# A DeltaNet layer followed by a gated feed-forward: first-layer steps as two tasks, quarter copies shared by two engines, and a new order of all tasks

## Chip, cores and metric

The kernel runs on one core of one Trainium2 chip. The metric is the device time of one execution in microseconds (us), the median of several runs; lower is better. A core has five engines that run side by side, each in the order of its own instruction list: TensorE (PE in the profile, its weight loads PEld), VectorE (DVE), ScalarE (ACT), GpSimd (POOL) and SyncE (SP, which here only issues DMAs).

## What is computed

```python
# attention: q, k, v of shape (4, 8, 768, 48), beta (4, 8, 768)
k_n = k / (norm(k) + 1e-6)
for t in range(768):
    y[t]  = q[t] @ state                       # state: 48 x 48 for each batch and head
    v_old = k_n[t] @ state
    state = state + beta[t] * outer(k_n[t], v[t] - v_old)
# feed-forward on x = y as 3072 tokens x 384
h = x @ w_in                                   # w_in: 384 x 2048
out = (h * cos(h)) @ w_out                     # w_out: 2048 x 384
```

All of it is float32; in the kernel the weights come in as 64-bit words and are made into float32 on the chip.

## The kernel before

**Chunks.** The 768 steps are cut into 24 chunks of 32 (`NU`, `C`). Within a chunk the recurrence is a triangular system. For each chunk n: `turn` transposes keys and queries (TensorE, L541, copied out by ScalarE at L555; from chunk 8 on by DMA and VectorE instead); `gram` multiplies them (L578), VectorE scales the product into `g` and `tt` (L589, L612); `inverse` inverts the triangular matrices of a pair of chunks column by column on GpSimd (L688, L695; the first pair on VectorE), going out to DRAM and back with `gram_put`, `gram_get`, `put` and `get` on SP's queue.

**The chain from chunk to chunk.** `state` (`through_state`, L745) multiplies the state so far by keys and queries into the PSUM tile `p_kq`. `old` (`old_values`, L757) copies the part that belongs to the keys into the tile `rhs`, four copies on ScalarE, one for each batch: a batch owns 32 of the 128 partitions (a quarter). `right` (`right_side`, L764) subtracts it from v on VectorE. The first four chunks solve in two halves: `solve_half` (L774), `half_out` (ScalarE, L784), `between` (L774), `between_out` (VectorE, L792), `solve` (L808); later chunks solve at once (L814). `solve_out` (VectorE, L822) makes u, `update` (L835) its product with the keys, `update_out` (VectorE, L845 for the first chunk, L843 after) adds that to the state. `within` (L852) finishes y in `p_kq`, and `within_out` (L865) copies it to the tile `y`, again in four quarters on ScalarE. The tiles `rhs` and `y` share one buffer. For the first four chunks `features` (L873) and `features_out` (ScalarE, L880) transpose y into the feed-forward's input `x_ffn`; later chunks go through VectorE and DRAM.

**Feed-forward.** Two chunks make a pair p of 256 tokens. Pairs 0 and 1 compute the first layer plainly: `hidden` (L924) fills one PSUM tile `p_h` of 128 x 512 with 12 matmuls, and there are 8 such steps for a pair, written (p, f) with f = 0, 2, ..., 14; f below 8 belongs to the pair's first chunk, the others to the second. A step's tile then goes through `turns` (ScalarE, L962), `rest` (VectorE, L969), `cos` (ScalarE, L978) and `gate` (VectorE, L987). Three PSUM banks (tag "h") hold such tiles. Pair 0's second layer is plain as well (`output`, L1130); all others use products of sums (`product`, L1187), and from pair 2 on the first layer is a chain of sums and products, too (`layer`, L1110). The sums of weights and of inputs are made on VectorE.

**Weights.** 28 loads (12 of `w_in`, 16 of `w_out`, `narrow_load`, L441) go through four buffers; each is worked on by `split` (ScalarE, L449, L451), `shift` (VectorE, L455, L460) and `add` (GpSimd, L464). `add` frees the buffer for a later load.

**Order.** Every piece of work is a task with a key, an engine, what it must follow, and the buffers that it makes and uses. The class `Order` takes a list of numbers, `LINE`, written out by hand or by a planner beforehand: the order in which all 2215 tasks are emitted. Each engine's own list is what remains of that order. The costs and due times given to `add` are for the planner; `Order.run` doesn't use them. It checks that a task's predecessors came before it and that buffers suffice. Where two engines touch one tile, the framework adds the waits; `pin` keeps each engine's instructions in the order emitted.

Of the kernel before, what the change touches and what calls it, by code (L numbers as in the profile page):

```python
# [197 lines left out]
def kernel(  # L198
# [45 lines left out]
    GATES = 8  # L244
    LEAD = 3
    MOVED = 4
    PLAIN_TURNS = 8
    DH = 32

    const = ctx.enter_context(tc.tile_pool(name="const", bufs=1))  # L250
# [28 lines left out]
    def by_parity(t):  # L279
        return t.rearrange("p (j a) i -> p a j i", a=2)  # L280
# [1468 lines left out]
```

## Time and profile before

| | us |
|---|---|
| runs, in order | 649.08, 651.08, 652.69 |
| median | 651.08 |
| profiled execution, whole | 655.38 |
| its span, first to last instruction | 653.3 |
| TensorE busy (10044 matmul records) | 596.1 |
| VectorE busy | 538.5 |
| ScalarE busy | 357.0 |
| GpSimd busy | 341.8 |

The span is what all views of the trace refer to; 2.1 us of the execution lie around it. A matmul of float32 shows as two records. The three runs and the profiled one are executions of one program, so a difference of one or two microseconds between single executions says nothing. The mean granted clock of TensorE was 0.993 of full speed. Of the span, TensorE is busy 91% and VectorE 82%.

### The profile page before, as it was taken

The numbers are of one execution on the slowest core, as the hardware profiler recorded it, in microseconds if no ns is written. First come the engines' busy times: TensorE is split into PE (matmuls) and PEld (weight loads), VectorE is DVE, ScalarE is ACT, GpSimd is POOL, SyncE is SP. The second block draws the span as 40 slices with busy tenths as digits, with TensorE's granted clock in tenths as the row PEclk, the third lists the DMA queues.
The fourth block names the chain that finished last, engine by engine and source line by source line (L and its number), as shares of the span: only waits on it lengthen the run. The fifth ranks groups of instructions, "written<-read, shape, count | busy, mean of one in ns | idle before, by whom it ended". The sixth has DMA issues, their size and how long they took to land.

```text
span 653.3 us, 24215 instructions
## 1 busy us (share of the span) xinstructions
PE 596.1 (91%) x10044; PEld 555.2 (85%) x10044; DVE 538.5 (82%) x1107; ACT 357.0 (55%) x658; POOL 341.8 (52%) x703
## 2 busy tenths in 40 slices
PE   4327868999999999999999999999999999999997
PEld 3216867887788999998999999999999999999996
DVE  6775666698989999999899999989998878778782
ACT  3434485774344565564666565655755646646340
POOL 5337457868847728738468487188681283000000
PEclk9999899999999999999999999999999999999999
DMA  8866745675465554534563545553413303110000
GB/s 187 188 120 163 185 100 115 148 143 83 86 106 83 104 90 84 100 75 82 99 108 71 119 65 106 103 91 71 93 38 67 78 15 66 43 39 25 1 25 24
DMA packets 237200, 58.65 MB, mean 90 GB/s; under 512 B 228644, under 2 KB 232116, under 8 KB 237092
## 3 DMA queue, kind: packets, MB, share of 16 engines
q1 hardware_dynamic: 234084, 56.24, 43.5%
q8 instruction: 79, 1.29, 0.8%
q10 hardware_dynamic: 2752, 0.43, 0.4%
q0 software_dynamic: 256, 0.44, 0.3%
q14 instruction: 29, 0.24, 0.1%
HBM read 42.65 MB, written 14.42 MB: 87 GB/s over the span
## 4 chain that ended last, share of the span: by engine, by line
PE 66%; DVE 13%; DMA 9%; ACT 5%; issue 3%; SPq 2%; POOL 1%; DVEq 0%; ACTq 0%; POOLq 0%
PE p_out L1187 23%; PE p_h L1110 23%; PE p_h L924 5%; PE p_kq L745 3%; PE p_s L835 3%; PE p_kq L852 2%; DVE p_h L1008 2%; PE p_u L814 2%; PE p_g L578 2%; DMA pairs<-in_moe_w_in_dram 2%; DMA z_dr<-z 1%; PE p_out L1130 1%; PE p_o L1187 1%; DVE g_ffn L987 1%; DVE turns L969 1%
## 5 line engine op out<-in xcount | busy, mean ns | idle before, releaser
L688 POOL TENSOR_TENSOR part<-z,gb 128x56 f32<-128x56 f32 (+25 forms) x325 | 130.8, 402 | 115.7 <-DMA gb<-g_dr 78.6
L695 POOL TENSOR_TENSOR z<-z,part 128x56 f32<-128x56 f32 (+25 forms) x325 | 136.9, 421 | 25.5
L1126 ACT COPY g_ffn<-p_h 128x512 f32<-128x512 f32 x140 | 78.9, 588 | 92.0 <-DVE p_h L1008 53.4
L1187 PE MATMUL p_out<-w_out,g_ffn 128*128 128x192 f32 x672 | 122.2, 329 | 0.6 <-DVE g L589 0.3
L1008 DVE TENSOR_TENSOR p_h<-p_h,g_ffn 128x512 f32<-128x512 f32 x140 | 96.8, 694 | 25.5 <-ACT g_ffn L1126 13.0
L1187 PEld LDWEIGHTS p_out<-w_out,g_ffn 128*128 128x128 f32 x672 | 107.8, 190 | 2.3 <-issue 0.5
L962 ACT ACTIVATE turns<-p_h,quarter_turn 128x512 int32<-128x512 f32 x96 | 66.0, 688 | 57.8 <-DVE p_h L1008 47.1
L1187 PE MATMUL p_out<-w_sum,g_ffn 128*128 128x192 f32 x496 | 90.8, 330 | 0.6 <-DVE o L1237 0.5
L978 ACT ACTIVATE turns<-turns,halfpi 128x512 f32<-128x512 f32 x96 | 69.1, 722 | 37.4 <-DVE turns L969 36.7
L1110 PE MATMUL p_h<-x_sum,w_in 128*128 128x128 f32 x640 | 83.4, 278 | 0.7 <-ACT g_ffn L1126 0.5
L1187 PEld LDWEIGHTS p_out<-w_sum,g_ffn 128*128 128x128 f32 x496 | 79.5, 190 | 1.9 <-DVE o L1237 0.9
L1110 PEld LDWEIGHTS p_h<-x_sum,w_in 128*128 128x128 f32 x640 | 78.1, 192 | 2.3 <-ACT g_ffn L1126 1.7
L969 DVE SCALAR_TENSOR_TENSOR turns<-p_h,turns 128x512 f32<-128x512 f32 x96 | 65.4, 682 | 9.6 <-ACT turns L962 8.8
L987 DVE TENSOR_TENSOR g_ffn<-turns,p_h 128x512 f32<-128x512 f32 x86 | 58.4, 679 | 9.2 <-ACT turns L978 9.2
L865 ACT COPY y<-p_kq 32x384 f32<-32x384 f32 x96 | 45.1, 470 | 37.5 <-PE p_kq L852 36.1
L1203 DVE TENSOR_TENSOR g_ffn<-g_ffn 128x512 f32<-128x512 f32 x88 | 61.9, 712 | 2.3 <-PE p_out L1187 2.2
L493 POOL TENSOR_TENSOR knrm<-ksum,halves 128x16 f32<-128x16 f32 (+1 forms) x14 | 37.5, 2682 | 35.6 <-DVE ksum L481 27.1
L1110 PE MATMUL p_h<-x_sum,in_sum 128*128 128x128 f32 x400 | 54.2, 278 | 0.5 <-DVE g_ffn L987 0.5
L1110 PEld LDWEIGHTS p_h<-x_sum,in_sum 128*128 128x128 f32 x400 | 49.6, 191 | 2.3 <-issue 1.5
L924 PE MATMUL p_h<-x_ffn,w_in 128*128 128x128 f32 x384 | 48.7, 286 | 2.1 <-ACT x_ffn L880 2.1
L924 PEld LDWEIGHTS p_h<-x_ffn,w_in 128*128 128x128 f32 x384 | 46.4, 200 | 3.4 <-ACT x_ffn L880 2.3
L757 ACT COPY rhs<-p_kq 32x384 f32<-32x384 f32 x92 | 43.1, 469 | 3.6 <-PE p_kq L745 2.6
(125 smaller groups left out, 876.1 us busy)
## 6 DMA issues: line engine op xcount, KB each, us to landing
pairs<-in_moe_w_in_dram SPq DMA_DIRECT2D x12, 512.0 KB
pairs<-in_moe_w_out_dram SPq DMA_DIRECT2D x16, 384.0 KB
gb<-g_dr SPq DMA_DIRECT2D x20, 256.0 KB
vp<-in_v_dram SPq DMA_DIRECT2D x96, 48.0 KB
out_dram<-o SPq DMA_DIRECT2D x23, 192.0 KB
y_dr<-y_t SPq DMA_DIRECT2D x20, 192.0 KB
x_ffn<-y_dr SPq DMA_DIRECT2D x40, 96.0 KB
kp<-in_k_dram SPq DMA_DIRECT2D x128, 24.0 KB
```

The source lines that it names most:

```text
L688: eng.tensor_tensor(out=part, in0=z[:, 0:rows, j, None].to_broadcast(shape), in1=a[:, j, None, j + 1 :].to_broadcast(shape), op=ALU.mult,)
L695: eng.tensor_tensor(out=behind, in0=behind, in1=part, op=ALU.subtract)
L924: nc.tensor.matmul(p_h[:, i], w_in[:, t, (4 * k + i) * 128 : (4 * k + i + 1) * 128], moved(p, t, unit), start=(t == 0), stop=(t == KT - 1),)
L962: nc.scalar.activation(turns[p, f], hidden_of(p, f), AF.Identity, bias=quarter_turn, scale=TURN)
L969: nc.vector.scalar_tensor_tensor(out=r, in0=hidden_of(p, f), scalar=TURN, in1=t, op0=ALU.mult, op1=ALU.subtract,)
L978: nc.scalar.activation(r, r, AF.Sin, bias=halfpi, scale=2.0 * math.pi)
L987: nc.vector.tensor_tensor(out=place(p, f), in0=step_of(rests.pop((p, f)), f), in1=step_of(hidden_of(p, f), f), op=ALU.mult,)
L1008: nc.vector.tensor_tensor(out=out, in0=one, in1=two, op=ALU.add if op == "add" else ALU.subtract)
L1110: nc.tensor.matmul(p_h[:, e], in_block(w)[:, e], form(p, x), start=first and e == 0, stop=True, skip_group_check=True,)
L1126: nc.scalar.copy(block(p, *CHAIN[i][3]), p_hs[p, BANK[i]])
L1187: nc.tensor.matmul(p_o, left(p, part, a)[:, e % 4], right(e, b), start=(e == 0), stop=(e == FT // 2 - 1), skip_group_check=True,)
L1203: nc.vector.tensor_tensor(out=left(p, s, to), in0=left(p, s, one), in1=left(p, s, two), op=op)
```

## The change

1. **Half steps.** `hidden` takes a further argument `part` and does two of its four 128-column blocks (6 matmuls). Each of the 16 steps of the two plain pairs becomes two tasks, which can stand apart on TensorE. The bank is taken by the first; `turns` follows the second.
2. **Shared quarter copies.** For chunks 0 to 3 (`SHARED = 4`) ScalarE copies only quarters 0 and 1 of old values (chunks 1 to 3) and of y (chunks 0 to 3). For quarters 2 and 3, VectorE subtracts old values straight from PSUM (two more instructions in `right`, whose last one then covers 64 rows in place of 128), and copies y out of PSUM (a new task `within_rest`, which `features` follows).
3. **Dependences dropped** from the task table: `eye` no longer follows `gram_put`; v of chunk 0, k and q of chunk 4, and `beta_home` no longer follow `gram_get` 0. They may be emitted earlier.
4. **Order.** `LINE` is a new list, of 2235 tasks.

```diff
+    SHARED = 4
...
     def old_values(n):
         rhs = rhss[n] = work.tile([128, H, D], FP, name="rhs", bufs=1)
-        for b in range(B):
+        for b in range(2 if n < SHARED else B):
             nc.scalar.copy(by_parity(rhs[quarter(b)]), p_kqs[n][quarter(b), :, b % 2])
...
-        nc.vector.tensor_tensor(out=rhss[n], in0=vt, in1=rhss[n], op=ALU.subtract)
+        rhs, rows = rhss[n], slice(0, 128)
+        if n < SHARED:
+            rows = half(0)
+            for b in range(2, B):
+                nc.vector.tensor_tensor(
+                    out=by_parity(rhs[quarter(b)]), in0=by_parity(vt[quarter(b)]),
+                    in1=p_kqs[n][quarter(b), :, b % 2], op=ALU.subtract,
+                )
+        nc.vector.tensor_tensor(out=rhs[rows], in0=vt[rows], in1=rhs[rows], op=ALU.subtract)
...
-    def within_out(n):
-        y = ys[n] = work.tile([128, H, D], FP, name="y", tag="rhs", bufs=1)
-        p_kq = p_kqs.pop(n)
-        for b in range(B):
-            nc.scalar.copy(by_parity(y[quarter(b)]), p_kq[quarter(b ^ 1), :, b % 2])
+    def within_out(n, bs=range(B)):
+        if n not in ys:
+            ys[n] = work.tile([128, H, D], FP, name="y", tag="rhs", bufs=1)
+        y, p_kq = ys[n], p_kqs[n]
+        for b in bs:
+            out, src = by_parity(y[quarter(b)]), p_kq[quarter(b ^ 1), :, b % 2]
+            if n < SHARED and b > 1:
+                nc.vector.tensor_copy(out, src)
+            else:
+                nc.scalar.copy(out, src)
...
-    def hidden(p, f):
+    def hidden(p, f, part):
         unit, k = f // 8, f // 2 % 4
-        p_h = p_hs[p, f] = bank("h", [128, 4, 128], "p_h")
-        for i in range(4):
+        if part == 0:
+            p_hs[p, f] = bank("h", [128, 4, 128], "p_h")
+        p_h = p_hs[p, f]
+        for i in range(2 * part, 2 * part + 2):
...
         add(("eye", m), "ACT", 0.65, lambda: invert_eye(m, held),
-            [("gram_put", 2 * m + 1)] + ([("eye", m - 1)] if m else []),
+            [("eye", m - 1)] if m else [],
...
-            if n == (0 if x == "v" else 4):
-                deps.append(("gram_get", 0))
...
+        shared = n < SHARED
+        add(("within_out", n), "ACT", 0.52, lambda: within_out(n, range(2 if shared else B)),
+            [("within", n)], makes=[("rhs", ("y", n))], uses=[("p_kq", n)])
+        if shared:
+            add(("within_rest", n), "DVE", 0.9, lambda: within_out(n, range(2, B)),
+                [("within_out", n)], uses=[("p_kq", n)])
...
-            layered[0] = ("hidden", p, f)
-            add(layered[0], "PE", 2.62, lambda f=f: hidden(p, f), deps,
-                makes=[("h", ("h", p, f))], uses=[("x", p)],
-                due=BASE[p] + f // 2 * (STEP if p else FIRST))
-            gating(p, f, [("hidden", p, f)], [("h", p, f)],
+            for part in range(2):
+                key = ("hidden", p, f, part)
+                add(key, "PE", 1.31, lambda f=f, part=part: hidden(p, f, part), deps,
+                    makes=[] if part else [("h", ("h", p, f))], uses=[("x", p)],
+                    due=BASE[p] + f // 2 * (STEP if p else FIRST))
+                deps = [key]
+            layered[0] = key
+            gating(p, f, [key], [("h", p, f)],
...
-    add(("beta_home",), "DVE", 0.8, spread_beta_home, [("beta",), ("gram_get", 0)])
+    add(("beta_home",), "DVE", 0.8, spread_beta_home, [("beta",)])
```

The list `LINE` itself isn't shown: its numbers stand for places in the table of tasks, which the change renumbers. What it moves around the first chunks is told where the prediction uses it.

More of the change, by code (lines that the diff above doesn't have):

```diff
@@ L1417, in unit @@
         add(("within", n), "PE", few, lambda: within(n), deps, uses=[("u", n), ("tt", n)])
-        add(("within_out", n), "ACT", 0.52, lambda: within_out(n), [("within", n)],
-            makes=[("rhs", ("y", n))], uses=[("p_kq", n)])
+        shared = n < SHARED
[4 more added lines that the diff above has]
+                [("within_out", n)], uses=[("p_kq", n)])
         if n >= MOVED:
@@ L1429, in unit @@
             return
-        add(("features", n), "PE", 0.33, lambda: features(n), [("within_out", n)],
+        add(("features", n), "PE", 0.33, lambda: features(n),
+            [("within_rest" if shared else "within_out", n)],
             makes=[("two", ("p_z", n))], uses=[("y", n)])
@@ L1631, in first_sums @@
     def first_sums():
-        plain_done = ("hidden", len(ONES) - 1, FT - 2)
+        plain_done = ("hidden", len(ONES) - 1, FT - 2, 1)
         made, read, homes = {}, {}, {}
```

203 rows, old and new, of the table LINE are left out of this document.

## Prediction, written before the changed kernel was run

> **What bounds the kernel now.** I read the slices of the page first, then the busy time by stretches, then the waits of TensorE in the stretches where it is not full.
>
> ```profile
> PE   4327868999999999999999999999999999999997
> DVE  6775666698989999999899999989998878778782
> PEclk9999899999999999999999999999999999999999
> ```
>
> A slice is 16.3 us. TensorE is short of full only in the first seven or so; from the ninth on it is full, and VectorE is nearly as full until the 27th. How much is open in each stretch:
>
> ```profile
> 0.00:63.00 63.00, 26.09 (x715) 21.57 (x715) 42.47 (x123) 25.46 (x57) 30.39 (x43) 1.00 0.75 162
> 63.00:93.00 30.00, 23.06 (x536) 21.41 (x526) 18.60 (x34) 19.61 (x40) 15.02 (x21) 0.94 0.68 159
> 93.00:160.00 67.00, 63.97 (x1375) 55.01 (x1375) 51.02 (x90) 43.37 (x86) 51.38 (x97) 1.00 0.59 122
> 160.00:250.00 90.00, 87.19 (x1464) 78.73 (x1460) 83.42 (x173) 43.73 (x80) 58.92 (x120) 0.98 0.53 94
> 250.00:600.00 350.00, 347.92 (x5658) 332.56 (x5658) 309.98 (x627) 208.59 (x372) 186.04 (x424) 1.00 0.39 75
> ...
> 63.08 1.22 PE L924 MATMUL p_h<-x_ffn,w_in 128*128 128x128 f32 x4
> ```
>
> The columns are the stretch, its length, and busy us of PE, PEld, DVE, ACT and POOL, then the clock; the last row is from the timeline (start, us). TensorE is idle 36.9 us up to 63 us, where the first hidden step starts, 6.9 in 63 to 93, 3.0 in 93 to 160, 2.8 in 160 to 250 and 2.1 in 250 to 600. The change adds and removes no matmul, so what it can win is idle time of TensorE and half-clock time. After 160 us there are 4.9 us to win, before it 46.8. VectorE has 11.4 us idle in 63 to 93, 16.0 in 93 to 160, 6.6 in 160 to 250: there the second engine has 7% left.
>
> **The half steps, 63 to 93 us.** What TensorE waits for in this stretch:
>
> ```profile
> PE p_h L924 <- ACT x_ffn L880: 2.1, 1, 2.1
> PE p_s L835 <- DVE u L822: 1.2, 1, 1.2
> PE p_g L578 <- ACT kq_t L555: 1.1, 1, 1.1
> PE p_z L873 <- DVE tt L612: 0.9, 1, 0.9
> PE p_kq L745 <- ACT y L865: 0.9, 1, 0.9
> PE p_u L808 <- DVE u_half L792: 0.7, 1, 0.7
> ```
>
> These are six stalls, from chunk 1's solve to step 8, 6.9 us together. A whole first-layer step lasts 2.84 us:
>
> ```profile
> 87.73 2.84 PE L924 MATMUL p_h<-x_ffn,w_in 128*128 128x128 f32 x24
> 78.28 1.56 PE L835 MATMUL p_s<-u,kp 64*64 64x96 f32 x32 [1.23 <-DVE u L822]
> 79.77 1.50 PE L852 MATMUL p_kq<-u,tt 32*32 32x48 f32 x64
> 84.33 1.20 ACT L555 COPY kq_t<-p_t 128x256 f32<-128x256 f32 x4
> 89.22 1.90 ACT L757 COPY rhs<-p_kq 32x384 f32<-32x384 f32 x4
> 92.68 0.49 PE L924 MATMUL p_h<-x_ffn,w_in 128*128 128x128 f32 x2 [2.11 <-ACT x_ffn L880]
> ```
>
> so a half step is 1.42 us, longer than five of the six. The changed kernel as built has on TensorE, from chunk 1's `between` on: a half step between `between` and `solve` (covers the 0.7), one between `solve` and `update` (the 1.2), and ahead of state 2 two halves, turn 5 and gram 5 (cover the 0.9 for y, and the 1.1 for kq_t: turn 5's copies, 1.20 us, have a half step beside them). Banks allow it: the three "h" banks hold steps 0, 2 and 4, and step 6 takes that of step 0, whose gate is then done. Two stalls stay. Features 1 still waits for `tt`, for VectorE now does a quarter-copy pair, a gate, a weight shift and a rest ahead of it: I take 0.8 of its 0.9. Step 8 still waits for `x_ffn`, with a cosine and a weight split ahead of it on ScalarE where the copies of old values (1.90 us) and a split stood before: I take 1.1 of its 2.1. Gain 6.9 - 1.9 = **5.0 us**.
>
> The stalls also cost clock:
>
> ```profile
> 78.15:81.56 3.41, 3.28 (x98) 2.97 (x99) 2.79 (x4) 0.22 (x1) 0.00 (x0) 0.50 0.86 188
> 128.10 0.89 PE L835 MATMUL p_s<-u,kp 64*64 64x96 f32 x32
> 128.92 0.88 PE L852 MATMUL p_kq<-u,tt 32*32 32x48 f32 x64
> ```
>
> Right behind the stalls at 75 to 78 us the granted clock is 0.50 for 3.41 us. Update and within took 1.56 and 1.50 us in it (above) against 0.89 and 0.88 later: 1.3 us lost, 1.5 with the start of the turn. With no gap there this goes: **1.5 us**. The Trainium skill (TensorE: Matmul & The Clock Gate, Part 1: The HAM clock gate) says the gate looks at windows of about 3.4 us, halves the clock after an idle one and gives it back after a busy one; the 3.41 us of the row agree. By that rule a new gap can bring the dip elsewhere, which is a rival below.
>
> **The start, 0 to 63 us.** The new order puts the inversion's identity ahead of the first gram's put, and the first V load earlier, but the first solve (it waited 10.9 us, first row) still stands behind the second V load, `weigh`, a fold, a shift and the `tt` of chunk 2 on VectorE, where a sum, the beta copies and two gram copies stood. I take 0 for it, between -1 and +1. What moves is here:
>
> ```profile
> PE p_w L774 <- DVE tt L612: 10.9, 1, 10.9
> ...
> 49.46 2.87 SPq L331 DMA_DIRECT2D qp<-in_q_dram  x4
> ...
> 51.59 0.55 DVE L504 TENSOR_TENSOR knrm<-knrm,tiny 128x16 f32<-128x16 f32 x1
> ...
> 54.77 0.69 DVE L455 SCALAR_TENSOR_TENSOR pairs<-pairs 128x512 uint32<-128x512 uint32 x1
> ...
> 55.71 0.95 DVE L845 COPY st<-p_s 128x768 f32<-128x768 f32 x1
> 63.20 0.42 DVE L589 TENSOR_TENSOR g<-p_g,bs 128x256 f32<-128x256 f32 x1 [6.54 <-PE p_g L578]
> ```
>
> The first state copy (L845), for whose bank turn 4 waits on TensorE, stands behind chunk pair 2's scales (51.59 to 54.8) and a shift. After the change the scales come behind it, in the 6.5 us in which VectorE idles. The shift stays ahead, and its weights are now issued behind the q load of chunk 4 (2.87 us of SP). So of the 3.2 us of scales at least 0.3 and at most all is won; beside what the q load costs the weights I take **1.0 us**.
>
> **The shared quarter copies.** Chunks 0 to 3: four pairs of copies of y and three of old values go from ScalarE to VectorE.
>
> ```profile
> L865 ACT COPY y<-p_kq 32x384 f32<-32x384 f32 x96 | 45.1, 470 | 37.5 <-PE p_kq L852 36.1
> L784 ACT COPY u_half<-p_w 128x384 f32<-128x384 f32 x4 | 1.9, 478 | 7.1 <-PE p_w L774 7.1
> L792 DVE TENSOR_TENSOR u_half<-rhs,p_v 128x384 f32<-128x384 f32 x3 | 1.6, 549 | 3.5 <-PE p_v L774 3.5
> L764 DVE TENSOR_TENSOR rhs<-vp,rhs 128x384 f32<-128x384 f32 x23 | 13.9, 602 | 2.2 <-ACT rhs L757 2.0
> ```
>
> ScalarE takes 470 ns over 32 partitions and 478 over 128, so an instruction is paid by columns. No row shows VectorE on 32 partitions; bounds are 0.14 us (a quarter of L792) and 0.60 (L764), and I take 0.55, that of L792, which also reads 384 columns of PSUM. That is 14 x 0.55 = 7.7 us more on VectorE; the 64-row subtraction left over still has 384 columns and costs its 0.60. ScalarE loses 14 x 0.47 = 6.6 us, which it has to spare. The chain is no shorter: in the changed kernel as built, VectorE's first quarter waits for ScalarE's second, since both write one tile. Old values and right side were 4 x 0.47 + 0.60 = 2.5 us and become 2 x 0.47 + 2 x 0.55 + 0.60 = 2.6.
>
> So these 7.7 us are a cost wherever VectorE is full. Chunk 0's pair (1.1) falls into the 6.5 us before 63. Chunk 1's two (2.2) fall into 63 to 93, which gets 6.5 us shorter: of 11.4 us idle, 11.4 - 6.5 - 2.2 = 2.7 stay. Chunks 2 and 3 (4.4) fall into 93 to 160, where 16.0 are idle. No stretch is overdrawn, but 63 to 93 is near it, and there VectorE meets GpSimd:
>
> ```profile
> 71.30 1.30 POOL L464 TENSOR_TENSOR w_in<-w_in,pairs 128x512 uint32<-128x512 uint32 x1 [2.10 <-DMA qp<-in_q_dram]
> 71.35 1.80 DVE L455 SCALAR_TENSOR_TENSOR pairs<-pairs 128x512 uint32<-128x512 uint32 x1
> ```
>
> The shift takes 1.80 us beside GpSimd's add and 0.69 alone: 1.1 us each time the two meet, and a fuller VectorE meets the adds more often. The Trainium skill (SBUF — State Buffer, SBUF: two separate sides) has it that a GpSimd instruction and a VectorE one with two SBUF inputs lock each other out whole; these rows agree, and by that rule the quarter copies, which read PSUM, are spared. I charge two more meetings on the path, **2.2 us** (from 0 to 7.7, all of the added work).
>
> **93 to 160 us and after.**
>
> ```profile
> PE p_s L835 <- DVE u L822: 1.7, 2, 1.2
> PE p_w L774 <- DMA vp<-in_v_dram: 0.7, 1, 0.7
> PE p_v L774 <- ACT u_half L784: 0.6, 1, 0.6
> ...
> PE p_u L814 <- DMA zt<-z_dr: 1.2, 1, 1.2
> 158.41 0.76 DVE L764 TENSOR_TENSOR rhs<-vp,rhs 128x384 f32<-128x384 f32 x1
> ```
>
> The first three are the 3.0 us of 93 to 160. Half steps now stand ahead of `between` 3 and `update` 2, and V is loaded earlier; but chunk 4's `u` and chunk 5's right side get more weight shifts and sums ahead of them on VectorE, and I leave 2.6: **0.4 us** won. After 160 us all tasks have new places and only 4.9 us are open; I allow one wait more like the longest there, **1.2 us** (from -2 to +5).
>
> **The sum.** -1.0 - 5.0 - 1.5 - 0.4 + 2.2 + 1.2 = -4.5 us. The profiled execution took 655.4 us (span 653.3) and would take 650.9; it lies 4.3 above the median of the three runs. A shift in the first 160 us carries over unchanged: 651.1 - 4.5 = **646.6 us**.
>
> **Rivals.**
> - *VectorE runs out of idle time (slower).* For it: 83.4 of 90 us busy in 160 to 250, and 7.7 us more ahead of that. Against it: 27.4 us idle before. It decides if less than 7.7 us of these are recovered. With only the scales' 3.0 us recovered, the end moves by 7.7 - 3.0 = 4.7, TensorE then waiting for VectorE in 160 to 250: 655.8 us.
> - *The stalls come back a step later (no change).* Half steps fill the gaps, but chunk 2's chain, not shorter, then finds fewer steps left, and TensorE idles before the outputs. Only the 1.0 of the start stays: 650.
> - *The clock dips again.* Nothing else goes wrong, but the two stalls left ahead of step 8 (1.9 us) halve the clock there: 1.5 back, 648.1. For it: the half-clock row above, with 1.9 us of stalls ahead of it. Against it: the 2.9 us of the three stalls between 82 and 88 us brought no dip. The Trainium skill's rule on the gate (the page and part named above) speaks against it, too, since 1.9 us do not fill a window.
> - *VectorE absorbs it all.* No charge of 2.2 or 1.2, and 0.8 more of the start: 646.6 - 4.2 = 642.4.
>
> **How the numbers follow.** Chances: forecast 0.38, VectorE short 0.22, stalls back 0.16, clock 0.10, all absorbed 0.14. About 0.5% (3.3 us) is what a measurement of this kernel can tell from no change. Forecast and full absorption lie below 647.8: faster 0.52. Clock and stalls lie within: 0.26. Slower 0.22. Low end: 3.2 + 6.9 + 1.5 + 0.4 = 12.0 without a charge, of which I take 11, since not all of it comes together: 640. High end: VectorE short, with the 1.2 on top: 657. Outside lies some 0.2, for waits after 160 us that no row of before can show.
>
> **What would show it.** In the changed profile the first hidden half should start near 62 us, step 8 near 85.5 instead of 92.7, with TensorE's idle time in 62 to 93 near 2 us and no half clock at 78. The quarter copies on VectorE should show 0.5 to 0.6 us each and begin after ScalarE's second. Chunk 5's right side should start near 153 (158.4 now). I am wrong if TensorE shows more than 4 us of idle time in 160 to 250 with VectorE as releaser, if the first half step starts after 63, or if the half steps wait for weights.

## The result, and the profile after

The changed kernel takes 646.93 us (median of 12 runs, 643.03 to 648.64) beside 652.77 for the kernel before (12 runs, 648.86 to 657.61): a ratio of 0.9909, with a 95% interval of 0.9886 to 0.9931, or 5.9 us less. Measured once more beside other kernels it gave 0.9901 (0.9863 to 0.9940). The forecast was 4.5 us less and a range of 640 to 657. The ratios, and the median of experiment 7, leave out two slow executions, one of that kernel (992.67 us at a granted clock of 0.56) and one of the kernel before (655.34 us).

The profiled execution of the changed kernel took 645.32 us, with a span of 643.4. The two profiles are thus 9.9 us of span apart and the medians 5.8: the profile before lay 2.6 us above its median of 12, that of after 1.6 below. What follows reads places from the profiles and sizes, where it can, from ratios of runs.

The slices of the page of the changed kernel (16.1 us each):

```profile
PE   4327889989999999999999999999999999999997
DVE  6875867888999999998999897999988977888782
PEclk9998999998999999999999999999999999999999
```

The sixth slice of TensorE has risen from 6 to 8, and it is full from the seventh on instead of the eighth. The clock row has its lower digits in other places. The same stretches as in the prediction (stretch, length, busy us of PE, PEld, DVE, ACT, POOL, then the clock):

```profile
0.00:63.00 63.00, 27.24 (x725) 22.76 (x726) 43.30 (x129) 25.50 (x55) 33.91 (x50) 0.97 0.76 162
63.00:93.00 30.00, 25.07 (x624) 23.25 (x624) 24.56 (x46) 20.04 (x42) 13.34 (x15) 1.00 0.71 162
93.00:160.00 67.00, 64.13 (x1318) 54.26 (x1322) 52.50 (x93) 37.80 (x72) 52.25 (x103) 0.97 0.63 129
160.00:250.00 90.00, 88.91 (x1576) 80.24 (x1568) 85.54 (x176) 46.65 (x85) 63.86 (x127) 1.00 0.52 92
250.00:600.00 350.00, 348.57 (x5575) 335.19 (x5567) 309.23 (x630) 210.07 (x372) 178.71 (x411) 1.00 0.39 74
```

Idle time of TensorE (length less the PE column), before and after: 36.9 and 35.8 us; 6.9 and 4.9; 3.0 and 2.9; 2.8 and 1.1; 2.1 and 1.4. So the stalls of 63 to 93 us gave 2.0, not 5.0, and the stretches behind 160 us gave 2.4 where the prediction feared a loss. Of the 9.9 us, 6.1 are idle time, and 3.8 are TensorE's busy time (596.1 to 592.3): the matmuls are the same, but some ran at another pace. Before, the 24 matmuls of the first step took 5.23 us, those of a later one 2.84; now 36 take 5.32 (below). The state product of chunk 1, just ahead of that step, shows the same, before and after:

```profile
58.61 1.96 PE L745 MATMUL p_kq<-st,kq_t 48*64 48x48 f32 x64
56.58 1.15 PE L747 MATMUL p_kq<-st,kq_t 48*64 48x48 f32 x64 [0.43 <-DVE y L878]
```

The update of chunk 0, ahead of both, took 1.56 us in both kernels, and a later one 0.89 (prediction). By such durations TensorE works at half pace in both up to some point, though the clock column prints 1.00 there: up to about 56 us in this profile, up to about 68 us in that of before. The order alone doesn't decide when the full pace comes. The kernels of experiments 3 and 12 have one and the same list up to 154 us; this product took 1.96 us in the one and 1.15 in the other, and the first step started at 63.2 and at 61.5. By the rows, some 2.5 of the 3.8 us of busy time come from this (an estimate: 0.8 for this product, 0.35 for the features, 1.4 for the first steps), the rest from the half clocks of later places.

What TensorE still waits for, in 62 to 93 us of the changed kernel (row: waiting operation, releaser, us in all, times, longest):

```profile
PE p_h L941 <- ACT x_ffn L895: 1.4, 1, 1.4
PE p_g L580 <- ACT kq_t L557: 1.4, 1, 1.4
PE p_w L784 <- DMA kp<-in_k_dram: 1.1, 1, 1.1
PE p_u L818 <- DVE u_half L802: 0.6, 1, 0.6
PE p_s L845 <- DVE u L832: 0.3, 1, 0.3
```

The waits for `u`, `tt` and `y` are filled or nearly so, as forecast; that for `u_half` is not (0.6, and 0.7 before). That for `kq_t` (the copies of turn 5) was to be covered by a half step and is not. ScalarE's timeline in the changed kernel says why (start, us, engine, line, operation, and in brackets the idle time ahead of it):

```profile
80.49 0.56 ACT L451 ACTIVATE w_out<-pairs 128x384 f32<-128x384 f32 x1 [1.31 <-DMA pairs<-in_moe_w_out_dram]
80.95 0.53 ACT L453 ACTIVATE pairs<-pairs 128x384 uint32<-128x384 uint32 x1
81.39 1.18 ACT L557 COPY kq_t<-p_t 128x256 f32<-128x256 f32 x4
```

Turn 5 was done at 79.9, but its copies stand behind a weight split that waited 1.31 us for its load. Two more of the five waits go back to such splits:

```profile
63.34 0.67 ACT L451 ACTIVATE w_in<-pairs 128x512 f32<-128x512 f32 x1 [3.62 <-DMA pairs<-in_moe_w_in_dram]
85.01 0.54 ACT L451 ACTIVATE w_out<-pairs 128x384 f32<-128x384 f32 x1 [1.25 <-DMA pairs<-in_moe_w_out_dram]
```

Ahead of chunk 1's solve the releaser named is a load of k, but the solve starts 0.2 us after the right side ends on VectorE (67.15), and the copies of old values that the right side needs stand behind the first of these splits. The feature copy that step 8 waits for was ready to run at 85.03 and starts at 85.89, behind the second. So about 3.3 of the 4.9 us (1.4, 1.1 and 0.8) are copies held by a split whose load came late. On TensorE:

```profile
60.89 5.32 PE L941 MATMUL p_h<-x_ffn,w_in 128*128 128x128 f32 x36
...
82.62 0.86 PE L580 MATMUL p_g<-kq_t 48*32 48x64 f32 x64 [1.35 <-ACT kq_t L557]
...
86.40 1.60 PE L941 MATMUL p_h<-x_ffn,w_in 128*128 128x128 f32 x12 [1.37 <-ACT x_ffn L895]
```

The first half step starts at 60.9 (62 forecast, 63.1 before), step 8 at 86.4 (85.5 forecast, 92.7 before), and chunk 5's right side on VectorE at 154.96 (153 forecast, 158.4 before). Part of the lead was lost on the way. The waits of TensorE in 93 to 160 us begin with

```profile
PE p_u L824 <- DMA zt<-z_dr: 1.7, 1, 1.7
```

the load of chunk 4's inverse, which no row of before had there; and a half clock stands right behind it. The copies, from the groups (count, busy us, mean ns, idle time ahead and its releaser), are as forecast, 0.56 us each, and wait for ScalarE's second quarter of the same tile:

```profile
L878 DVE COPY y<-p_kq 32x384 f32<-32x384 f32 x8 | 4.5, 559 | 2.4 <-ACT y L880 2.3
L770 DVE TENSOR_TENSOR rhs<-vp,p_kq 32x384 f32<-32x384 f32 x6 | 3.3, 556 | 4.1 <-ACT rhs L759 4.0
```

### The profile page after: what moved, and what is told of

It reads as the page before. It is cut to its first block, busy times and chain, and to the rows that moved or that the text cites. A ratio compares the mean times of both kernels' runs of the same rounds, so it can differ in the third digit from the quotient of the medians.

```text
span 643.4 us, 24201 instructions
## 1 busy us (share of the span) xinstructions
PE 592.3 (92%) x10044; PEld 552.7 (86%) x10044; DVE 542.1 (84%) x1121; ACT 351.5 (55%) x644; POOL 342.1 (53%) x703
## 4 chain that ended last, share of the span: by engine, by line
PE 73%; DMA 8%; DVE 6%; SPq 4%; POOL 4%; issue 2%; ACT 2%; DVEq 0%; ACTq 0%; POOLq 0%
PE p_out L1204 28%; PE p_h L1127 28%; PE p_kq L747 3%; SPq L333 3%; PE p_s L845 3%; PE p_kq L862 2%; DMA pairs<-in_moe_w_in_dram 2%; PE p_u L824 2%; PE p_out L1147 2%; PE p_g L580 2%; PE p_o L1204 2%; DMA pairs<-in_moe_w_out_dram 2%; POOL part L690 1%; PE p_h L941 1%; POOL z L697 1%
## 5 line engine op out<-in xcount | busy, mean ns | idle before, releaser
L690 POOL TENSOR_TENSOR part<-z,gb 128x56 f32<-128x56 f32 (+25 forms) x325 | 134.1, 412 | 107.9 <-DMA gb<-g_dr 54.0
L697 POOL TENSOR_TENSOR z<-z,part 128x56 f32<-128x56 f32 (+25 forms) x325 | 134.0, 412 | 25.5
L1204 PE MATMUL p_out<-w_out,g_ffn 128*128 128x192 f32 x672 | 120.9, 328 | 0.0
L880 ACT COPY y<-p_kq 32x384 f32<-32x384 f32 x88 | 41.4, 470 | 22.8 <-PE p_kq L862 21.6
L941 PE MATMUL p_h<-x_ffn,w_in 128*128 128x128 f32 x384 | 49.5, 285 | 1.5 <-ACT x_ffn L895 1.4
L1127 PE MATMUL p_h<-x_ffn,w_in 128*128 128x128 f32 x320 | 42.6, 278 | 0.8 <-ACT g_ffn L1143 0.8
```

The lines of the kernel that those rows point to most:

```text
L690: eng.tensor_tensor(out=part, in0=z[:, 0:rows, j, None].to_broadcast(shape), in1=a[:, j, None, j + 1 :].to_broadcast(shape), op=ALU.mult,)
L697: eng.tensor_tensor(out=behind, in0=behind, in1=part, op=ALU.subtract)
L941: nc.tensor.matmul(p_h[:, i], w_in[:, t, (4 * k + i) * 128 : (4 * k + i + 1) * 128], moved(p, t, unit), start=(t == 0), stop=(t == KT - 1),)
L1127: nc.tensor.matmul(p_h[:, e], in_block(w)[:, e], form(p, x), start=first and e == 0, stop=True, skip_group_check=True,)
L1204: nc.tensor.matmul(p_o, left(p, part, a)[:, e % 4], right(e, b), start=(e == 0), stop=(e == FT // 2 - 1), skip_group_check=True,)
```

## Experiments

My theory after the result: the half steps and the start carry the gain, the shared copies cost a little. Rivals: the sharing carries it, or the order behind 160 us does. All ratios are to the kernel before, run beside each. Where a diff shows names of tasks, these are entries of `LINE`, in which nothing else is moved.

**1. Whole steps in the new order.**

```diff
-hidden.p.f.0 ... solve.n, turn.n, ... hidden.p.f.1
+hidden.p.f.0 hidden.p.f.1 ... solve.n, turn.n, ...      (all 16 steps)
```

> The changed kernel with the two halves of every first-layer step put together again, both in the place of the first half; the shared copies and the rest of the new order stay. If the halves are what fills the stalls of 62 to 93 us, they come back behind the solve, the update and the gram of chunks 1 and 5: 2 to 4 us more idle time there, step 8 later by as much, and 649 to 651 us beside 646.9 of the changed kernel. Rival, the gain is that of the shared copies and of the rest of the order: idle time as in the changed kernel (4.9 us) and 647 us.

649.3 us, ratio 0.9960 (0.9935 to 0.9986): 2.6 us below before instead of 5.9, so the halves are worth 3.3 us in the new order, as the theory has it (the two intervals don't overlap). In 62 to 93 us TensorE is idle 6.7 us, beside 4.9 in the changed kernel and 6.2 in a second profile of it (experiment 6): less than the 2 to 4 us more that I expected there. The waits in 93 to 160 us of this kernel begin with

```profile
PE p_u L818 <- DVE u_half L802: 1.4, 2, 0.7
PE p_s L845 <- DVE u L832: 1.2, 1, 1.2
PE p_t L543 <- DVE st L853: 1.2, 1, 1.2
```

TensorE is idle 5.4 us in that stretch, beside 2.9 in the changed kernel. These are stalls that half steps fill, but they lie in the chains of chunks 2 and 3, later than the prediction put them.

**2. Two steps halved, in the order of before** (copies by ScalarE alone; the halves of the other steps stay together).

```diff
-hidden.0.4.0 hidden.0.4.1 ... between.1 ... solve.1
+hidden.0.4.0 ... between.1 ... solve.1 hidden.0.4.1
-turn.5 ... state.2 ... gram.5 ... features.1 ... hidden.0.6.0 hidden.0.6.1
+turn.5 hidden.0.6.0 ... state.2 hidden.0.6.1 ... gram.5 ... features.1
```

> The kernel before with two steps halved and nothing else changed (copies by ScalarE alone, order of before): the second half of the third step behind the solve of chunk 1, the fourth step's halves behind the turn of chunk 5 and behind the state product of chunk 2. Of the stalls of before it covers 1.2 us ahead of the update, and 0.9, 1.1 and 0.9 us ahead of the state product, the gram and the feature transposes: 4.1 us. If the halves carry the gain, 2 to 4 us below before, the fifth step at 88 to 90 us beside 92.7. Rival, the stalls come back a step later (the feature copy that the fifth step waits for): the fifth step at 92 and within 1 us of before.

654.3 us, ratio 1.0038 (1.0015 to 1.0061): 2.5 us slower. The theory fell here; the rival has the place right, and put the time within 1 us of before. TensorE's timeline of this kernel and then ScalarE's:

```profile
87.21 0.52 PE L888 MATMUL p_z<-consts,y 128*128 128x128 f32 x3 [0.97 <-DVE tt L614]
92.52 5.49 PE L941 MATMUL p_h<-x_ffn,w_in 128*128 128x128 f32 x24 [4.79 <-ACT x_ffn L895]
```

```profile
88.43 0.72 ACT L995 ACTIVATE turns<-turns,halfpi 128x512 f32<-128x512 f32 x1 [2.53 <-DVE turns L986]
89.06 1.90 ACT L759 COPY rhs<-p_kq 32x384 f32<-32x384 f32 x4
90.98 0.55 ACT L451 ACTIVATE w_out<-pairs 128x384 f32<-128x384 f32 x1
91.44 0.52 ACT L453 ACTIVATE pairs<-pairs 128x384 uint32<-128x384 uint32 x1
91.98 0.48 ACT L895 COPY x_ffn<-p_z 128x384 f32<-128x384 f32 x1
```

The stalls of 75 to 87 us are filled. What was won is then waited for at once ahead of step 8 (4.79 us in place of 2.1): the feature copy of chunk 1 was ready to run at 87.7, and in the old order of ScalarE it stands behind a cosine that waits for VectorE, the copies of old values and a weight split. Step 8 starts at 92.5, as before. Behind that wait the clock is half:

```profile
91.43:98.26 6.83, 5.74 (x27) 5.75 (x28) 4.83 (x14) 4.75 (x11) 3.40 (x12) 0.50 0.56 124
```

Step 8's 24 matmuls take 5.49 us here and took 2.94 before, so in this profile the loss is one of pace behind the wait. Whether it is so in the other executions stays open: their mean granted clock is 0.991, that of the kernel before beside them 0.992. In the new order the same copy starts at 85.89, ahead of the next cosine and the copies of old values. These two halved steps lose in the old order, and the halves gain in the new one; that ScalarE's list makes the difference is read from the rows and wasn't tried by itself.

**3. Shared copies alone, in the order of before** (constant 4, whole steps, `within_rest` behind `within_out`).

> The kernel before, its order and its whole steps, with the quarter copies of chunks 1 to 3 shared and nothing else changed. The prediction charged 2.2 us (0 to 7.7) for the sharing: 653 to 655 beside 652.9 of the kernel before, the chain of chunks 1 to 3 within 0.5 us of its old length. Rival, sharing is worth something by itself: 651 or less.

653.61 us, ratio 1.0044 (1.0014 to 1.0075): 2.9 us slower, where I had charged 2.2. The stretches 93 to 160 and 160 to 250 us:

```profile
93.00:160.00 67.00, 62.87 (x1348) 54.60 (x1349) 54.51 (x97) 41.19 (x82) 48.39 (x94) 1.00 0.59 124
160.00:250.00 90.00, 86.21 (x1431) 77.33 (x1433) 82.97 (x173) 43.85 (x80) 60.02 (x121) 1.00 0.53 93
```

TensorE is idle 4.1 us in 93 to 160 and 3.8 in 160 to 250, beside 3.0 and 2.8 before: 2.1 us more. VectorE is busier by 3.5 us in 93 to 160 (54.5, 51.0 before). The path is not the one that I charged for. The profile has one weight shift of 1.8 us beside an add, as before, and no further one of that size. What grew is the wait ahead of step 8, from 2.1 to 3.7 us. ScalarE and TensorE there:

```profile
92.49 0.54 ACT L451 ACTIVATE w_out<-pairs 128x384 f32<-128x384 f32 x1 [2.58 <-DMA pairs<-in_moe_w_out_dram]
93.48 0.48 ACT L895 COPY x_ffn<-p_z 128x384 f32<-128x384 f32 x1
94.02 2.94 PE L941 MATMUL p_h<-x_ffn,w_in 128*128 128x128 f32 x24 [3.69 <-ACT x_ffn L895]
```

VectorE's copies of y stand ahead of a sum that GpSimd needs (83.74, 80.83 before); GpSimd's weight add behind it starts 2.9 us later (87.88, 84.96 before), the load for which that add frees the buffer is issued at 88.92 (87.39 before), and the split ahead of the feature copy waits for that load.

**4 and 5. One engine for the copies, in the new order**, twice.

```diff
-    SHARED = 4
+    SHARED = 0
```

> The changed kernel with ScalarE making all four quarter copies again (constant 4 to 0), halves and order as they are. My theory is that the sharing buys nothing: VectorE loses 7.7 us of work and ScalarE gets 6.6 us, the chain of chunks 1 to 3 stays within 0.5 us per chunk, and the time is 645 to 647 us, the same as or up to 2 us below the changed kernel. Rival, the sharing carries the gain by relieving ScalarE: the copies of chunks 1 to 3 then come later, and 649 us or more.

> The changed kernel with ScalarE making all four quarter copies, once more, beside the changed kernel on one chip. If the sharing costs 1 to 3 us, as the shared copies alone did to the kernel before (1.0044, 2.9 us), this is 1 to 3 us below the changed kernel. Rival, in the new order the shared copies are hidden: within 1 us.

645.1 us, 0.9883 (0.9851 to 0.9915), and 644.0 us, 0.9893 (0.9849 to 0.9938); the changed kernel had 0.9909 and, beside the second, 645.5 us and 0.9901. Below it both times, by 1.7 and 0.5 us after the ratios, with intervals that overlap. That the sharing carries the gain is excluded; that it costs something in the new order is likely, not shown. TensorE's idle time in 93 to 160 us points the same way: 0.9 and 1.0 us in these two profiles, 2.9 and 1.9 in the two of the changed kernel.

**6. The changed kernel again.**

> The changed kernel once more, for a comparison on one chip with the other runs of this call. 0.991 of before; its profile tells whether the half clock at 145 us and the 1.7 us wait for chunk 4's inverse are in every execution (rival: the half clocks fall in other places, as they did in the other runs' profiles, at 84 to 93 us).

645.49 us. The half clocks lie elsewhere. From the profile of the first execution and from that of this one:

```profile
59.69:63.10 3.41, 3.32 (x74) 3.15 (x75) 1.61 (x4) 0.04 (x1) 2.94 (x8) 0.50 0.88 208
145.02:148.44 3.42, 3.42 (x71) 2.97 (x74) 2.65 (x6) 0.00 (x0) 2.62 (x9) 0.50 0.44 57
```

```profile
68.92:72.33 3.41, 3.41 (x48) 3.19 (x52) 3.38 (x5) 1.58 (x4) 2.59 (x2) 0.50 1.02 285
85.98:92.81 6.83, 5.74 (x32) 5.25 (x33) 5.67 (x14) 2.90 (x6) 1.01 (x1) 0.50 0.66 130
```

6.8 us at half clock in one, 10.2 in the other, of one program. The wait for chunk 4's inverse is 0.8 us here instead of 1.7, that ahead of chunk 1's solve 3.2 instead of 1.1. So neither the half clock at 145 us nor the 1.7 us belongs to the kernel as such.

**7 and 8. Chunk 4's inverse loaded early**, with shared copies and with ScalarE alone.

```diff
-put.2 blocks.8.0 gram_put.7 weights.27 get.4 gram_get.3
+put.2 get.4 gram_put.7 weights.27 gram_get.3 blocks.8.0
```

> The changed kernel with SyncE's queue changed at 131 to 143 us: the load of chunk 4's inverse right behind its store, and the load of the blocks of chunk 8 behind the Gram load of pair 3. Its profile lost 3.0 us of its lead there: 1.7 us in which TensorE waited for that load, and a half clock of 3.4 us right behind. Theory: both go, and with them 2 to 3.4 us: 643.5 to 645 us. Rival, another wait of chunk 4 or 5 takes the place or the half clock comes anyway: less than 1 us, 646 to 647.

> The same change of SyncE's queue, with ScalarE making all four quarter copies. It was 645.1 us without the change of the queue (1.8 below the changed kernel, intervals overlapping). If the sharing costs 1 to 2 us and the early load gains 2 to 3, this is the best of all, 642 to 644 us, 1 to 2 below the run with the early load alone. Rival, the sharing is worth nothing either way: the same as the run with the early load alone.

643.87 us, 0.9911 (0.9885 to 0.9938), and 643.74 us, 0.9906 (0.9873 to 0.9940): by the ratios no gain on the changed kernel (the kernel before had 651.09 beside these two). In the profile of experiment 7 TensorE no longer waits for this load. But SyncE's timeline shows that the load is issued no earlier:

```profile
132.67 0.44 SPq L711 DMA_DIRECT2D z_dr<-z  x1
137.24 1.80 SPq L730 DMA_DIRECT2D zt<-z_dr  x4
```

Right behind the store, the load is still issued only 4.6 us after it, at 137.24 (137.33 in the changed kernel, where the store was issued 1.4 us earlier): SyncE waits 4.0 us for the store to land, in place of the DMA issues of 5.3 us that stood between. Chunk 4's solve came 1.1 us later (142.27, 141.16 in the changed kernel), and the load was there by then. The rival with little gain holds.

**9. The scales moved back.**

```diff
+scale.2.0                                  (ahead of shift.8)
 shift.8 ... update_out.0 ... within_rest.0
-scale.2.0
```

> The changed kernel with one task moved back: the scales of chunk pair 2 ahead of the shift of weight tile 8 and of the first state copy on VectorE, as before. The prediction gave this move 1.0 us; the profiles show 2.5 at the turn of chunk 4 (56.72 to 54.18). If the move is what the start gains, the turn of chunk 4 comes 2 to 2.5 us later, the first half step at 62.5 to 63, and the end 1 to 2 us later than the changed kernel beside it. Rival, the start gains by the rest of its order (shifts, copies): the turn of chunk 4 within 0.5 us of 54.2 and the end unchanged.

645.31 us, 0.9899 (0.9859 to 0.9938), beside 645.49 for the changed kernel: the move is worth nothing that can be measured. Turn 4 starts at 55.0 (54.2 and 54.5 in the two profiles of the changed kernel, 56.7 before). So my cause for the start was wrong. VectorE's timeline for the scales, of before and then of this kernel:

```profile
52.17 1.22 DVE L506 TENSOR_TENSOR krec<-knrm 128x16 f32<-128x16 f32 x1
53.42 0.25 DVE L507 RECIPROCAL krec<-krec 128x16 f32<-128x16 f32 x1
53.71 0.92 DVE L509 TENSOR_TENSOR bs<-bt,krec 128x16 f32<-128x16 f32 x1
```

```profile
51.86 0.17 DVE L506 TENSOR_TENSOR knrm<-knrm,tiny 128x16 f32<-128x16 f32 x1
52.06 0.17 DVE L508 TENSOR_TENSOR krec<-knrm 128x16 f32<-128x16 f32 x1
52.27 0.25 DVE L509 RECIPROCAL krec<-krec 128x16 f32<-128x16 f32 x1
52.56 0.17 DVE L511 TENSOR_TENSOR bs<-bt,krec 128x16 f32<-128x16 f32 x1
```

and GpSimd's timeline of before at that time:

```profile
50.82 3.77 POOL L464 TENSOR_TENSOR w_in<-w_in,pairs 128x512 uint32<-128x512 uint32 x3 [4.06 <-DVE w_in L460]
```

The five operations of the scales (the four here and one of 0.19 us behind them) take 1.1 us in all here and took 3.3 before in the same place. Before, three weight adds ran back to back beside them, from 50.82 on, 1.26 us each: they end at 52.1, 53.3 and 54.6. The two-input operations of the scales end at 52.14 (the one at 51.59, quoted in the prediction), 53.39 and 54.63, each just behind an add; the reciprocal between them takes its 0.25 us in both. In the new order the tiles of the weights are spread otherwise: here one add ends at 51.60 and the next starts at 53.98, with the scales between. The Trainium skill (SBUF — State Buffer, SBUF: two separate sides) says that GpSimd and a VectorE operation with two SBUF inputs lock each other out; the rows agree. The profiles of experiments 2, 3 and 12, which have the old start, show the 1.22 us of the second operation as well. That the start gains by the spread adds is read from these rows, and wasn't tried by itself.

**10 and 11. The new order up to 89 us, and up to 154 us**, with that of before behind (shared copies; whole steps behind the seam).

```diff
-LINE of the changed kernel
+its tasks up to turn.6 (10) or right.5 (11), then the others as in before
```

> The new order up to the turn of chunk 6 (the first 240 of 2235 tasks, up to about 89 us), and behind it the order of before, with steps whole and the shared copies kept. If the gain is made at the start and in the stalls of 62 to 93 us, nearly all of it is here: the lead at 93 us is that of the changed kernel (6 us), and the end is 646 to 648 us. Rival, the later part of the new order carries it: the lead at 93 us stays or is lost, and 650 us or more.

> The new order up to the right side of chunk 5 (about 154 us), and behind it the order of before. Theory: nothing more is gained behind 160 us than a half clock of 1.7 us that before shows at 194 us, and the end is 646 to 648 us, within 1 us of the changed kernel. Rival, the order behind 160 us is worth 3 us or more, by the idle time that the two profiles show there (1.1 us beside 2.8, and 1.4 beside 2.1): 650 us.

Experiment 10 took 658.19 us, 1.0073 (1.0048 to 1.0099), and failed as an experiment: at the seam TensorE waits 6.9 us for turn 6's copies, which ScalarE's old list puts behind a weight split whose load came late. It says nothing on the part behind, only that a list can't be joined there. Experiment 11 took 649.5 us, 0.9945 (0.9920 to 0.9969): 2.3 us short of the changed kernel.

**12. The order of before up to 154 us, the new one behind** (shared copies, whole steps ahead of the seam).

```diff
-LINE of experiment 3
+its tasks up to right.5, then the others as in the changed kernel
```

> The counterpart of the run that had the new order up to 154 us (0.9945 of before, beside 0.991 of the changed kernel): the order of before up to the right side of chunk 5, steps whole, copies shared, and the new order behind it. If the order behind 160 us is worth the 2.5 us that the two runs leave for it, this comes out 2 to 3 us under the run with the shared copies alone, with its lead made between 160 us and the end. Rival, that part is worth nothing by itself and the difference of the two runs is their spread: within 1 us of the shared copies alone.

650.09 us, 0.9990 (0.9967 to 1.0012), against 1.0044 with shared copies alone: the order behind 154 us is worth 3.5 us here, and 2.3 by experiment 11. TensorE's waits in 158 to 210 us in the kernel of experiment 3 (old order) are

```profile
PE p_u L824 <- DMA zt<-z_dr: 1.7, 1, 1.7
PE p_u L824 <- DVE rhs L774: 0.5, 1, 0.5
```

that is, chunk 6 waits for its inverse and for its right side; in the changed kernel 0.2 us of these is left. TensorE's idle time in 160 to 210 us goes from 2.5 (experiment 3) to 1.4 in this kernel and 0.2 in the changed one.

The profiles of all kernels bear out this gain. From the start of chunk 5's right side to the end of the span, the five with the old order there take 491.4 to 494.9 us, the nine with the new one 487.3 to 489.5. That right side itself starts at 158.4 to 160.1 us with the old order ahead of it (before, experiments 2, 3 and 12), at 159.0 with the new order and whole steps (experiment 1), and at 155.0 and 156.1 in the changed kernel.

## Why the prediction was right, point by point

The total was near (4.5 forecast, 5.9 measured), but by terms that were off on both sides, so that it came as near as it did is in part luck: ahead of 160 us the forecast had 7.9 us of gain without the charge for sharing, and the runs give 5.3 up to 154 us; behind it the forecast had a loss of 1.2, and the runs give a gain of 2.3 to 3.5.

- **Start, 1.0.** Turn 4 came 2.5 and 2.2 us earlier in the two profiles of the changed kernel, the first half step 2.2 and 2.9; part of the latter may be the pace of the start, which the prediction didn't price. The step failed in its cause: "the first state copy stands behind the scales" is true, but their place is worth nothing (experiment 9); what went is the 2.2 us by which GpSimd's adds stretched them. I had a row of that (0.55 us for 16 columns) and read it as the length of the work. That GpSimd's adds explain it is read from rows (experiment 9).
- **Half steps, 5.0.** Mis-sized: 3.3 by experiment 1. In the two profiles 4.9 and 6.2 us stay idle where I left 1.9. The cover for `kq_t` failed (1.4 us): the half step lay there, but the copies it was to cover were held by a weight split. The 0.7 for `u_half` was to be covered, and 0.6 stays. The solve of chunk 1 has a wait of 1.1 (3.2 in the second profile) that before had not, behind a split as well. And the term is not the halves' alone: two halved steps in the old order lose 2.5 us (experiment 2). The prediction saw ScalarE's new order at step 8 and priced it at 1.0 us; with the old one the sign was another.
- **Half clock gone, 1.5.** Failed as it was argued. The dip at 78 us went, and others came: by the clock column 6.8 us at half clock in the profile of before (from 78.15 and 194.21 us), 6.8 and 10.2 in the two of after, up to the last matmuls. What TensorE won in pace, 3.8 and 3.5 us of busy time, lies for the greater part in the half pace of the start, which this count leaves out and the prediction didn't price. The rival "the clock dips again" had the fact right, and the place in most profiles: of the ten with the new order around gram 5 and step 8, six (experiments 1, 4, 5, 6, 7 and 11) show 6.8 or 10.2 us of half clock that begin between 83.6 and 86.2 us. In these the wait for `kq_t` just ahead was 1.5 to 2.5 us, in the four without a dip there 1.0 to 1.4. So dips came behind waits that fill no window, which the prediction took as speaking against that rival.
- **93 to 160, 0.4.** Right in size (0.1 and 1.1 us less idle time in the two profiles), with a new wait of 1.7 or 0.8 us for chunk 4's inverse where the old ones went.
- **Shared copies, charge of 2.2.** Right in size: 2.9 (0.9 to 4.9) in the old order, 0.5 and 1.7 in the new. Duration and order of the quarters were as forecast. The path was not: no second shift of 1.8 us beside an add shows, and the delay runs through a sum, GpSimd's adds and a weight load to the feature copy (experiment 3).
- **After 160 us, charge of 1.2.** Wrong in sign: 2.3 to 3.5 us won. The wait for chunk 6's inverse stood in the prediction's rows; I should have asked of the new order whether it stays.
- **Rivals.** VectorE did not run short: TensorE's waits for it in 160 to 250 us come to 0.2 us, of 1.1 idle. That the stalls come back a step later is what the two halved steps do in the old order.

Four runs make a chain from the kernel before to the changed one in which each differs from the last in one thing (but for a few tasks at the seam of experiment 12): sharing +2.9 us (experiment 3, 1.0044); the order behind 154 us -3.5 (experiment 12, 0.9990); the order ahead of 154 us, with whole steps, -2.0 (experiment 1, 0.9960); the halves -3.3 (the changed kernel, 0.9909). Each step is known to some 2 us, and that of 2.0 is not clear of nothing, since its two intervals overlap. The pieces depend on the order in which they are put on, as experiment 2 shows.

## What to carry to other kernels

Filling a stall on the full engine pays only if the next thing that it waits for moves up as well: look in the helper engine's list for what stands ahead of that releaser (here often a split that waits for its load), and price the two together. An instruction of another engine that is several times longer than its like elsewhere may be contention and not work: ask what ran beside it before moving it. A half clock seen in one profile is no term of a sum unless a second profile of the same program shows it in the same place.

## What the runs showed of the hardware

- VectorE's two-input operations of 16 columns took 0.17 us between GpSimd's adds and up to 1.22 us beside them (experiment 9).
- VectorE takes 0.56 us for 384 columns out of PSUM on 32 partitions, beside 0.55 on 128 (prediction); ScalarE, 0.47 on both. A copy cut by partitions was not cheaper here.
- The granted clock was half in stretches of 3.41, 6.83 and (experiment 4) 10.24 us, one to three times the same length, in different places in two executions of one program. The stretch at 145.02 us had TensorE busy all through (3.42 us) and stands behind a single gap of 1.68 us. The Trainium skill (TensorE: Matmul & The Clock Gate, Part 1: The HAM clock gate) has the clock halved after an idle window of about 3.4 us. The lengths agree with such windows; the gap ahead of 145 us, half a window, does not, and I can't say what decided it. Other gaps don't settle it: one of 4.79 us ended in half clock (experiment 2) and one of 3.69 did not (experiment 3), while six dips at 84 to 86 us came behind gaps of 1.5 to 2.5 us.
- Between the DRAM store of chunk 4's inverse and the issue of the load behind it lie 3.5 us on SyncE's queue in the kernel before (133.69 to 137.16), with other issues between, and 4.6 us in experiment 7 with none, of which SyncE waited 4.0 for the store.
- The time at which TensorE came to full pace in the first 70 us differed between kernels with one and the same list (experiments 3 and 12, the state product in 1.96 and 1.15 us).
